# A ring of four slots instead of five for streamed weights

## The chip, the cores and the metric

The kernel runs on one core of one Trainium2 chip. The metric is the device time of one execution in microseconds (us). The kernel before was run three times: 1899.77, 1908.93 and 1909.86 us, median 1908.93.

## The reference

The layer mixes two branches, token by token: `out = g*a + (1-g)*b` with `g = sigmoid(sum(x * gate_w))`. Branch b is a feed-forward net with a gated GELU (2048 tokens of width 640, inner width 1536). Branch a is a recurrence over 64 segments of 32 tokens, and it is where the time goes:

```python
for s in range(n_seg):                      # 64 segments
    xs = x[:, s * seg_len:(s + 1) * seg_len, :].copy()
    h = jnp.concatenate([mem, xs], axis=1)  # 8 memory rows + 32 tokens
    q = jnp.einsum('btd,dhe->bhte', h, Wq)  # 32 heads of 192
    k = jnp.einsum('btd,dhe->bhte', h, Wk)
    v = jnp.einsum('btd,dhe->bhte', h, Wv)
    ...                                     # masked softmax
    o = jnp.einsum('bhqk,bhke->bhqe', p, v)
    o = jnp.einsum('bhte,hed->btd', o, Wo)
    mem = o[:, :M, :].copy()                # feeds the next segment
```

The eight memory rows of a segment come out of the segment before it, so segments can't overlap, and each of them reads all of Wq, Wk, Wv and Wo.

## The kernel before

**Stages.** First the feed-forward branch runs in four blocks of 512 tokens and leaves its rows in DRAM. Then the "left" stage (line 852) computes Q and K for the last eight tokens of each segment, for all segments at once. Then the 64 segments run one after the other; this is the recurrent stage, from about 316 us on.

**A segment.** The heads are treated in four octets. The list `PROG` gives the order of a segment's steps: `q`, `k` (line 931) and `v` (line 951) project an octet, `sc`, `ex` and `pt` compute scores, softmax and transposed probabilities, `pv` (line 1071) applies them to V, and `wo` (line 1094) multiplies with the rows of Wo and sums into one PSUM bank. At the end of a segment line 1139 copies the sum out, line 1149 transposes the new memory rows, and line 1154 puts them where the next segment's projections read them. An instruction scheduler written in Python (`_Sched`) turns declared reads and writes of memory regions into semaphore waits; each engine gets its operations in program order.

**Weights as pieces.** The four matrices don't fit into SBUF together, so they are cut into 84 pieces: 20 each of Wq, Wk and Wv (one 128-row slab for one octet, 128 x 3072 bytes, 384 KB) and 24 of Wo (two rows of 128, 128 x 2560 bytes, 320 KB). Below, "Q 0,3" is the Wq piece of octet 0, slab 3. Two pieces are held elsewhere (in PSUM, copied back on ACT at lines 610 and 623). The others are *resident* (loaded once, at line 647) or *streamed* (loaded again in each segment).

**Who is streamed.** A planner decides it when the kernel is built. It walks through `PROG` with a cost for each step (`COST`, in us) and so gives each piece a time of use. It then raises the number of streamed pieces, `nstream`, until the rest fits into `res_cap`, the bytes left after the work buffers and the ring. For each `nstream` it spreads target times evenly over a segment and takes for each target the allowed piece whose use lies nearest. One byte of the ring is one byte fewer for resident pieces:

```python
ring_bytes = B_RING * GQ                    # GQ = 3072 bytes a partition
res_cap = total - wsA_total - wsB_total - ring_bytes
```

**The ring.** Streamed pieces go through `B_RING` slots in turn. `issue_ring` (line 567) declares a DMA on the SP queue that writes slot `n % B_RING`. It has to wait until TensorE has finished with the piece that was in the slot before, and TensorE's matmuls wait for its landing. The SP queue is in order, and in the recurrent stage it carries nothing else but, in the first segment, late loads of resident pieces. The left stage passes ten pieces through the same slots (line 635). Other transfers, the rows of x, the left Q and K, b and the output, are issued by ACT (line 678 and 907).

In the kernel before, a segment streams 20 pieces through five slots: 4 of Wq, 5 of Wk, 3 of Wv and 8 of Wo.

Of the kernel before, what the change touches and what calls it, by code (L numbers as in the profile page):

```python
# [221 lines left out]
def _build(nc, A_x, A_mem0, A_Wq, A_Wk, A_Wv, A_Wo, seg_len, w_gate, w_up, w_down,  # L222
           gate_w, out, opts=None):
    opts = dict(opts or {})
# [81 lines left out]
    ffn_sz["brow"] = al(NBR * Dm * 2)  # L306
    ffn_total = sum(ffn_sz.values())

    B_RING = int(opts.get("ring", 5))
    ring_bytes = B_RING * GQ  # L310
    res_cap = total - wsA_total - wsB_total - ring_bytes
    assert total - wsA_total - ffn_total >= ring_bytes
# [7 lines left out]
    assert ffn_base >= ring_bytes  # L320
    ring_off = [j * GQ for j in range(B_RING)]
    o = wsA_base - wsB_total
# [137 lines left out]
    def piece_src(key):  # L460
        if key[0] == 3:
            r0, r1 = wo_row(2 * key[1]), wo_row(2 * key[1] + 1)
            return bass.AP(Wo2.tensor, Wo2.offset + r0 * Dm, [[3 * Dm, 128], [(r1 - r0) * Dm, 2], [1, Dm]])
        m, o_, k = key
        return (Wq2, Wk2, Wv2)[m][:, k, OW * o_:OW * (o_ + 1)]
# [4 lines left out]
    def piece_view(key, o):  # L470
        if key[0] == 3:
            return bview(o, GO).rearrange("p (c n) -> p c n", n=Dm)
        return bview(o, GQ)
# [55 lines left out]
    stream_list = [i for i in range(npieces) if i in streamed]  # L529
    assert nstream >= B_RING  # L530
    res_off = {}
# [30 lines left out]
    def issue_ring(seg, upto):  # L562
        done = issued.get(seg, 0)
        while done <= upto:
            key = order[stream_list[done]]
            slot = stream_counter[0] % B_RING
            S_.add("sp", lambda e, slot=slot, key=key: e.dma_start(piece_view(key, ring_off[slot]), piece_src(key)),
# [63 lines left out]
    def issue_left(upto):  # L631
        while len(left_slot) <= upto:
            key = left_stream[len(left_slot)]
            slot = stream_counter[0] % B_RING
            S_.add("sp", lambda e, slot=slot, key=key: e.dma_start(piece_view(key, ring_off[slot]), piece_src(key)),
                   writes=[r_ring[slot]], dma_sem="ring%d" % slot, name="ring left")
            stream_counter[0] += 1
            left_slot[key] = slot
# [11 lines left out]
    def load_residents(cls):  # L650
        for key in order:
            if key in res_off and slot_class[key] == cls:
                load_resident(key)
# [89 lines left out]
    def ffn_transposes(blk):  # L743
        s = blk % 2
        fns = []
        for a in range(FA):
            for k in range(KT):
                bank = k // 2
                col = (k % 2) * FB + a * 128
                fns.append(lambda e, a=a, k=k, bank=bank, col=col:  # L750
                           e.transpose(psb(bank)[:, col:col + 128], xr_sb[s][:, a, k * 128:(k + 1) * 128], ident))
        nb = (KT + 1) // 2
        S_.add("pe", fns, reads=[r_xr[s], r_ident], writes=[r_ps[b] for b in range(nb)], name="ffn xT %d" % blk)
        for bank in range(nb):
            k0 = 2 * bank
            nk = min(2, KT - k0)
            eng = "dve" if bank % 2 == 0 else "act"
            src = psb(bank)[:, 0:nk * FB].rearrange("p (k s t) -> p k s t", k=nk, t=L)
            dst = xT_sb[:, k0:k0 + nk]
            rk = [sreg(ffn_off["xT"] + 2 * k * L, 2) for k in range(k0, k0 + nk)]  # L760
            if eng == "dve":
                S_.add("dve", lambda e, src=src, dst=dst: e.tensor_copy(out=dst, in_=src),
                       reads=[r_ps[bank]], writes=rk)
            else:
                S_.add("act", lambda e, src=src, dst=dst: e.activation(out=dst, in_=src, func=ACTF.Copy),
                       reads=[r_ps[bank]], writes=rk)
        ns = FB // L
        aux_dma(xts[blk * ns:(blk + 1) * ns].rearrange("s p c -> p s c"),
                xT_flat.rearrange("p (s c) -> p s c", c=KT * L), r_xT, [Rg("xt", blk * ns, (blk + 1) * ns)], "xts")
# [50 lines left out]
    ffn_transposes(0)  # L820
    issue_left(min(B_RING, len(left_stream)) - 1)
    load_residents(0)
# [353 lines left out]
    for s in range(NSEG):  # L1176
# [5 lines left out]
                ring=B_RING, arena_bytes=arena_bytes,  # L1182
# [25 lines left out]
def bass_gated_mix__memory_aug_recurrent_mem_tr__glu_gated_geglu__prompt_kernel(  # L1208
    nc,
    A_x,  # L1210
    A_mem0,
    A_Wq,
    A_Wk,
    A_Wv,
    A_Wo,
    A_seg_len,
    B_x,
    B_w_gate,
    B_w_up,
    B_w_down,  # L1220
    gate_w,
    out,
):
    _build(nc, A_x, A_mem0, A_Wq, A_Wk, A_Wv, A_Wo, A_seg_len, B_w_gate, B_w_up, B_w_down, gate_w, out)
# [33 lines left out]
```

## Time and profile before

| what | value |
|---|---|
| profiled execution | 1908.93 us |
| its span, first to last instruction | 1907.2 us |
| mean granted TensorE clock | 0.983 |
| matmuls busy (PE) | 1762.1 us, 92% |
| weight loads busy (PEld) | 1126.8 us, 59% |
| VectorE, ScalarE busy | 929.6 us, 874.6 us |
| packets of the SP queue | 506.45 MB, 77.6% of 16 engines' span |
| packets of the ACT queue | 39.48 MB, 7.6% |

How to read it: the profile is one execution taken by the hardware profiler. PE and PEld are the matmuls and the weight loads of TensorE; both are fed by one sequencer. Matmuls are pipelined and their ends are modelled, so that PE counts as busy for longer than its array works. "Idle before" or "waited for" is an engine's idle time, put down to what ended it. In the chain of waits the program's last instruction is followed back, at each step to what released it. A DMA's landing is the moment when its last share has raised the semaphore. The time from issue to landing holds everything between, also the wait behind other transfers.

The transfers by origin in the page: Wo 528 issues of 320 KB, median 4.5 us to landing; Wk 340, Wq 277 and Wv 209 of 384 KB, 5.1, 4.9 and 5.1 us.

### The profile page before, as it was taken

What the parts mean: (1) busy time and instruction counts of PE and PEld (TensorE: products, weight loads), DVE (VectorE), ACT (ScalarE), POOL (GpSimd) and SP (SyncE); (2) the same over time, 40 slices, a digit from 0 to 9 for tenths busy, and PEclk for the clock granted to TensorE, in tenths of its full rate; (3) what the DMA queues carried; (4) which work ended last, traced back from release to release, by engine and by line L of the source; (5) the groups of instructions that cost most, each with busy time, mean ns of one, the idle gap of its engine ahead of it and who ended that gap; (6) DMA issues with size and microseconds to landing.
All of it is one profiled execution on the core that took longest, in us unless ns stands there. A gap on an engine that the chain in (4) does not pass through costs nothing.

```text
span 1907.2 us, 78849 instructions
## 1 busy us (share of the span) xinstructions
PE 1762.1 (92%) x34421; PEld 1126.8 (59%) x34429; DVE 929.6 (49%) x2890; ACT 874.6 (46%) x2045; POOL 145.1 (8%) x547
## 2 busy tenths in 40 slices
PE   7999995899999999999999999999999999999998
PEld 3454443566666666666666666666666566666665
DVE  3222332455555555555555555555555455545555
ACT  2222332444555454545454545455545444445554
POOL 1000000000000000000000000000000000000000
PEclk9999997999999999999999999999999999999999
DMA  9511567999999998999999999999999999999998
GB/s 373 196 35 41 153 162 247 329 310 314 304 304 326 304 325 301 322 311 331 312 317 308 308 309 331 311 327 313 321 307 324 301 315 310 308 308 316 325 319 276
DMA packets 280422, 550.98 MB, mean 289 GB/s; under 512 B 82434, under 2 KB 106506, under 8 KB 280074
## 3 DMA queue, kind: packets, MB, share of 16 engines
q1 hardware_dynamic: 201386, 506.45, 77.6%
q10 hardware_dynamic: 78688, 39.48, 7.6%
q8 instruction: 269, 4.41, 0.9%
q14 instruction: 79, 0.65, 0.1%
HBM read 524.69 MB, written 21.10 MB: 286 GB/s over the span
## 4 chain that ended last, share of the span: by engine, by line
PE 66%; DMA 24%; DVE 4%; ACTq 3%; issue 1%; ACT 1%; SPq 0%; DVEq 0%
PE ps L931 19%; DMA arena<-in_A_Wo_dram 13%; PE ps L1094 11%; PE ps L951 11%; DMA arena<-in_A_Wv_dram 5%; PE ps L852 4%; PE ps L1071 4%; DMA arena<-in_A_Wq_dram 4%; PE ps L993 3%; PE ps L785 3%; PE ps L782 3%; ACTq L867 2%; DMA arena<-in_A_Wk_dram 2%; PE ps L800 2%; PE ps L985 2%; PE ps L975 1%
## 5 line engine op out<-in xcount | busy, mean ns | idle before, releaser
L931 PE MATMUL ps<-arena 128*32 128x384 bf16 x10240 | 516.5, 334 | 29.2 <-DVE arena L1154 16.3
L1094 PE MATMUL ps<-arena 128*40 128x320 bf16 x6144 | 479.8, 300 | 30.6 <-DMA arena<-in_A_Wo_dram 26.3
L1094 PEld LDWEIGHTS ps<-arena 128*40 128x40 bf16 x6144 | 308.1, 100 | 135.8 <-DMA arena<-in_A_Wo_dram 65.7
L935 ACT ACTIVATE arena<-ps 128x384 bf16<-128x384 f32 x512 | 311.6, 609 | 148.6 <-PE ps L931 130.4
L931 PEld LDWEIGHTS ps<-arena 128*32 128x32 bf16 x10240 | 254.7, 98 | 173.1 <-DVE arena L1154 20.8
L951 PE MATMUL ps<-arena 128*32 128x384 bf16 x5800 | 294.6, 332 | 4.0 <-DMA arena<-in_A_Wv_dram 3.0
L941 DVE STREAM_TRANSPOSE arena<-arena 128x192 f32<-128x192 f32 x512 | 190.1, 371 | 120.8 <-ACT arena L935 120.2
L610 ACT ACTIVATE arena<-ps 128x576 bf16<-128x576 bf16 (+1 forms) x192 | 113.4, 590 | 234.7 <-PE ps L1094 231.7
L951 PEld LDWEIGHTS ps<-arena 128*32 128x32 bf16 x5800 | 147.6, 98 | 93.5 <-DMA arena<-in_A_Wv_dram 9.1
L962 ACT ACTIVATE arena<-ps 128x384 bf16<-128x384 f32 x256 | 125.6, 491 | 161.6 <-PE ps L951 79.5
L911 POOL COPY arena<-arena 128x96 bf16<-128x96 bf16 x256 | 68.4, 267 | 1555.6 <-PE ps L993 825.4
L1048 DVE TENSOR_TENSOR arena<-ps,arena 128x320 bf16<-128x320 bf16 x256 | 125.6, 491 | 114.7 <-PE ps L1045 112.8
L1020 ACT ACTIVATE ps<-ps 104x160 f32<-104x160 f32 x256 | 72.9, 285 | 176.8 <-DVE ps L1010 176.2
L1071 PEld LDWEIGHTS ps<-arena 128*64 128x64 bf16 x3072 | 113.0, 125 | 59.3 <-DVE ps L1010 25.8
L1075 ACT ACTIVATE arena<-ps 128x320 bf16<-128x320 f32 x256 | 111.7, 436 | 73.3 <-PE ps L1071 72.0
L1071 PE MATMUL ps<-arena 128*64 128x160 bf16 (+1 forms) x3072 | 136.4, 222 | 7.7 <-ACT arena L623 3.5
L1139 DVE CAST arena<-ps 104x320 bf16<-104x320 f32 x63 | 31.0, 492 | 228.5 <-PE ps L1094 228.5
L993 PE MATMUL ps<-arena 64*40 64x40 bf16 (+1 forms) x4096 | 120.6, 181 | 1.9 <-issue 1.7
L1008 DVE TENSOR_REDUCE arena<-ps 104x4 f32<-104x160 f32 x256 | 81.2, 317 | 72.2 <-PE ps L993 72.1
L852 PE MATMUL ps<-arena 128*128 128x512 bf16 x480 | 104.3, 380 | 4.2 <-ACT arena L859 4.2
L993 PEld LDWEIGHTS ps<-arena 64*40 64x40 bf16 (+1 forms) x4096 | 100.2, 97 | 11.5 <-issue 2.6
L1022 DVE TENSOR_REDUCE arena<-ps 104x4 f32<-104x160 f32 x256 | 82.3, 322 | 46.7 <-ACT ps L1020 27.7
(73 smaller groups left out, 1494.8 us busy)
## 6 DMA issues: line engine op xcount, KB each, us to landing
arena<-in_A_Wo_dram SPq DMA_DIRECT2D x528, 320.0 KB, 4.5
arena<-in_A_Wk_dram SPq DMA_DIRECT2D x340, 384.0 KB, 5.1
arena<-in_A_Wq_dram SPq DMA_DIRECT2D x277, 384.0 KB, 4.9
arena<-in_A_Wv_dram SPq DMA_DIRECT2D x209, 384.0 KB, 5.1
left_qk_scratch<-arena ACTq DMA_DIRECT2D x16, 768.0 KB, 8.1
arena<-left_qk_scratch ACTq DMA_DIRECT2D x64, 192.0 KB, 4.9
arena<-in_A_x_dram SPq DMA_DIRECT2D x4, 640.0 KB, 15.1
xt_scratch<-arena ACTq DMA_DIRECT2D x4, 640.0 KB, 9.1
```

Of the source, the lines that this page charges most:

```text
L610: S_.add("act", lambda e: e.activation(out=bview(o_held2, GQ)[:, c0:c1], in_=psb(b)[:, p0:p0 + c1 - c0], func=ACTF.Copy), reads=[r_ps[b]], ...
L852: S_.add("pe", [lambda e, k=k, g_=gs[k][0], i=i, bk=bk: e.matmul(ps[:, bk, 0:NL].rearrange("p (g t) -> p g t", t=L), g_[:, i * 128:(i + 1) ...
L931: S_.add("pe", [lambda e, j=j, k=k, gv=gv: e.matmul(ps[32 * j:32 * j + 32, bank, 0:384].rearrange("p (c i) -> p c i", i=32), Hb[hb][:, k, ...
L935: S_.add("act", lambda e: e.activation(out=rows_sb[m].rearrange("p (b i h) -> p b h i", b=6, h=2), in_=ps[:, bank, 0:384].rearrange("p (b ...
L941: S_.add("dve", lambda e: e.transpose(out=dst[:, :, 0:L], in_=rows_sb[m].bitcast(F32).rearrange("p (c r) -> p c r", r=L)), reads=[r_rows[m ...
L951: return [lambda e, j=j: e.matmul(ps[32 * j:32 * j + 32, bk, 0:384], lhs, g_[:, 384 * j:384 * (j + 1)], start=(k == 0), stop=(k == KT - 1) ...
L962: S_.add("act", lambda e: e.activation(out=v_sb[o % NVB], in_=ps[:, bank, 0:384], func=ACTF.Copy), reads=[r_ps[bank]], writes=[r_v[o % NVB ...
L993: fns.append(lambda e, gp=gp, lo=lo, hi=hi, b=(3 * tl + c) // 2, h=(3 * tl + c) % 2, tl=tl, last=(c != 1): e.matmul(ps[gp:gp + R, bank, tl ...
L1048: S_.add("dve", lambda e: e.tensor_tensor(out=PTm, in0=apx(pv[:, 0:104], [[64, 2], [0, 4], [1, R]]), in1=apx(mbd, [[0, 2], [1, 4], [0, R]] ...
L1071: fns.append(lambda e, lhs=lhs, left=left, h=h, dst=dst, rhs=rhs: e.matmul(dst, lhs, rhs, start=not left, stop=left, tile_position=(0, 64 ...
L1075: S_.add("act", lambda e: e.activation(out=apx(u[:, 0, 0, :], [[R, 2], [3 * R, 4], [1, R]]), in_=ps[:, A, 0:2 * W].rearrange("p (c t r) -> ...
L1094: fns.append(lambda e, g_=g_, i=i, c=c, h=h, tl=tl, cc=cc, u=u: e.matmul(ps[64 * h:64 * h + R, OB, 0:HD], u[:, tl, cc, :], g_[:, i, HD * h ...
```

## The change

The default number of ring slots goes from five to four. Nothing else in the text of the kernel changes; the planner, which computes with `ring_bytes`, then chooses another set of resident and streamed pieces, and slots follow in turns of four.

```diff
-    B_RING = int(opts.get("ring", 5))
+    B_RING = int(opts.get("ring", 4))
     ring_bytes = B_RING * GQ
     res_cap = total - wsA_total - wsB_total - ring_bytes
     assert total - wsA_total - ffn_total >= ring_bytes
```

The loop that the number feeds, unchanged:

```python
nstream = 0
while True:
    streamed = set()
    for k in range(nstream):
        target = (k + 0.5) * tseg / nstream
        best = min((i for i in range(npieces) if i not in streamed and i not in held_i and may_stream(order[i])), key=lambda i: abs(tcons[i] - target))
        streamed.add(best)
    if tot_bytes - GO - GQ - sum(piece_size(order[i]) for i in streamed) <= res_cap:
        break
    nstream += 1
```

The streamed pieces of a segment, in order of use:

| slots | pieces |
|---|---|
| five (20) | Q 0,3; K 0,4; Q 1,1; K 1,0; K 1,4; Q 2,3; K 2,1; V 2,0; Q 3,1; K 3,0; V 3,0; V 3,4; Wo 2, 5, 8, 11, 15, 18, 21, 23 |
| four (19) | Q 0,4; K 0,4; Q 1,2; K 1,1; Q 2,0; Q 2,4; K 2,3; V 2,2; Q 3,4; K 3,3; V 3,2; Wo 0, 5, 6, 11, 14, 18, 21, 23 |

## The prediction

> **What bounds the kernel now.** I read the page first: its span, engine shares and chain of waits.
>
> ```profile
> span 1907.2 us, 78849 instructions
> PE 1762.1 (92%) x34421; PEld 1126.8 (59%) x34429; DVE 929.6 (49%) x2890; ACT 874.6 (46%) x2045; POOL 145.1 (8%) x547
> ...
> PE 66%; DMA 24%; DVE 4%; ACTq 3%; issue 1%; ACT 1%; SPq 0%; DVEq 0%
> ```
>
> TensorE (PE) is nearly always busy, yet 24% of the chain is the flight of weight transfers. So weights arrive just in time. The busy time by stretches says whether bandwidth is short (columns end with granted clock, DMA share, GB/s):
>
> ```profile
> 0.00:50.00 50.00, 39.25 (x278) 19.27 (x280) 14.91 (x27) 12.81 (x19) 5.28 (x25) 1.00 0.99 374
> ...
> 345.00:1900.00 1555.00, 1457.19 (x32121) 974.57 (x32118) 832.66 (x2714) 780.06 (x1897) 134.71 (x504) 0.99 0.93 314
> ```
>
> The recurrent stage, 345 to 1900 us, is four fifths of the run. There the DMA engines look 0.93 occupied but move 314 GB/s; with a deep queue (first 50 us) they moved 374. So the stage uses 84% of a rate that this run shows. Next, the line that issues ring transfers: who waits for it, and issue to landing.
>
> ```profile
>   PEld ps L1094: 65.7, 124
>   PE ps L1094: 26.3, 42
>   PEld ps L931: 24.1, 40
>   PE ps L931: 10.9, 14
>   PEld ps L951: 9.1, 19
>   PEld ps L1071: 4.1, 6
>   PE ps L1071: 3.2, 5
>   PE ps L951: 3.0, 7
> ...
> DMA to landing us min/median/max: 3.1/4.8/10.6
> ```
>
> Matmuls idle 43.4 us for ring transfers, weight loads 103.0 us (partly covered by matmuls still running). The SP queue's own waits, and one piece of the chain, say why landings are late:
>
> ```profile
> SPq L567 <- PE ps L931: 299.4, 224, 17.0
> ...
> SPq L567 <- PE ps L1094: 178.8, 200, 1.8
> ```
>
> ```profile
> 1077.88 0.48 PE ps L931 x9
> 1078.36 6.04 DMA arena<-in_A_Wv_dram
> 1084.40 0.04 issue
> 1084.45 0.35 PE ps L951 x4
> ```
>
> SP waits for a matmul to finish with a slot, issues at once, and 6.04 us later TensorE goes on at the landing. The loop "slot freed, issue, landing, use" is what is tight. Last, the segment's length, from one instruction per segment:
>
> ```profile
> L1139 DVE CAST arena<-ps x63: 490/492/493, 352.2 to 1879.3; 104x320 bf16<-104x320 f32 x63
> ```
>
> (1879.3 - 352.2) / 62 = 24.63 us.
>
> **The change part by part.** By the planner's arithmetic (the issue counts of the page, 528 + 340 + 277 + 209 = 1354 = 64 x 20 + 10 + 62 + 2, confirm it for five slots) the 3072 bytes of the fifth slot make one more piece resident: 19 streamed instead of 20, 63 resident instead of 62. The streamed set is spread anew: 5 Wq, 4 Wk, 2 Wv, 8 Wo (was 4, 5, 3, 8).
>
> *Removed:* 64 SP issues of 0.33 us and 64 x 384 KB. SP spends its time waiting, so the issues are worth nothing. The bytes are hidden unless bandwidth is the bound (rival below). *Added:* one resident load, 384 KB at 374 GB/s = 1.1 us, issued while the FFN runs and the DMA share falls to 0.24 (50 to 180 us): nothing. If that cover were gone it would cost its 1.1 us. *Left stage:* ten left-row pieces pass the smaller ring, each needed two or more groups of about 13 us after its slot is free; landings there take 3.1 to 4.1 us: nothing.
>
> *Queues:* every ring issue now waits for the matmul four pieces back instead of five. Behind it on SP stand only further ring issues (and, in segment 0, late resident loads), so what is late is the landing, and TensorE waits for that. ACT's DMA queue and POOL are not passed.
>
> *The ring itself.* Average first. A slot's turn took 5/20 x 24.63 = 6.16 us; landing 4.8, reading 0.34 (Q, K, V) to 0.45 (Wo) and 0.09 for issue and semaphore make some 5.3, so 0.9 us was spare. With four slots a turn is 4/19 x 24.63 = 5.19 us: nothing is spare at the old landing time.
>
> Now piece by piece. From the instruction records I took, over segments 4 to 63, the median time from each piece's first matmul to the next one's where that one had landed 0.15 us early or more: a segment without ring stalls, 23.1 us. From it follows each streamed piece's window, from the last read of the piece before it in its slot to its own use. Windows with four slots, by turns of the ring (us):
>
> - Q, K, Q, K: 4.71, 4.44, 4.92, 5.59
> - Q, Q, K, V: 4.48, 4.32, 4.36, 4.42
> - Q, K, V, Wo: 4.22, 4.90, 4.87, 4.85
> - Wo x4: 4.95, 4.27, 4.44, 4.19
> - Wo x3: 3.92, 4.08, 3.18
>
> With five slots the shortest of the four turns were 5.26, 5.13, 5.43 and 3.99 (the last Wo piece).
>
> A landing plus 0.09 must fit the window; the largest excess in a turn is its stall (a stall early in a turn lengthens the later windows of the same turn, so they aren't added). Landings now average 4.95 (Q, K, V) and 4.52 (Wo): only 4.61 - 3.99 = 0.62 us per segment is overdue on average; the other 0.1 to 1.0 of the 0.7 to 1.6 measured (43.4 and 103.0 over 64) is scatter (standard deviation of a landing 0.63). I leave that scatter as it is.
>
> What will a landing take? Sorted by how many ring transfers were in flight at issue: four, 5.10 (Q, K, V) and 4.72 (Wo); three, 4.88 and 4.43; two, 4.13 and 4.31. With four slots a transfer meets three at most.
>
> - Slow end: the mean over three and fewer, 4.76 and 4.41. Stalls 0.41 + 0.53 + 0.63 + 0.31 + 1.32 = 3.20, or 2.58 more than 0.62; over 63 segments +163 us.
> - Fast end: the rows of two, 4.13 and 4.31. Stalls 0 + 0 + 0 + 0.21 + 1.22 = 1.43; +51 us.
> - Taken: 4.45, the middle, for Q, K, V, because "three in flight" in a ring of five often means that a fourth has just gone through the same engines; for Wo 4.27, a little under its row of two, because the Q, K, V transfers ahead of it thin out too. Stalls 0.10 + 0.22 + 0.32 + 0.17 + 1.18 = 1.99, so 1.37 more, x 63 = +86 us.
>
> The profiled execution took 1908.93 us (span 1907.2 and 1.7 around it), which is also the median of the three runs: 1908.9 + 86 = 1995 us.
>
> The Trainium skill ("Perfetto Trace Analysis", Identifying the Most-Contended Engine) judges a DMA by its HBM utilization and calls occupancy misleading. Read by occupancy, 0.93, the saved bytes would be worth the 69 us of the first rival; read by rate, 314 of 374 GB/s, they are worth nothing. The same skill ("DMA: Bandwidth & Descriptors", Anatomy of one DMA) gives 2.0 us plus bytes at 436 GB/s for a transfer issued from GpSimd; by that, an estimate, 384 KB land in 2.9 us, every window holds, and the sum would be -0.62 x 63 = -39 us. This trace's 4.8 us median speaks against it, its 3.1 us minimum for it.
>
> **The rivals.**
>
> *DMA bandwidth is the bound (faster).* For: share 0.93. Against: 314 against 374 GB/s, and SP waiting for TensorE before every issue. If so, the segment shortens by the removed transfer's engine time. A 3072-byte packet took 141 ns on average and each of 16 engines carries eight: 1.1 us, x 63 = -69, 1840 us. It decides where landings fall to 3.56 us: then the last window, 3.18, leaves 0.47 us of stall instead of 0.62, which is 9.5 us over 63 segments; for the full price they must come down to the 3.1 of a lone transfer.
>
> *Relief pays for the slot (same).* Landings of about 3.9 leave stalls of 0 + 0 + 0 + 0 + 0.81, near the 0.62 of now: +12 us, 1921; at 3.7, 1908. For: isolated transfers land in 3.1 to 3.3 us. Against: even with two in flight, 4.1 to 4.3.
>
> *No relief (slower still).* Landings stay 4.95 and 4.52: stalls 0.60 + 0.72 + 0.82 + 0.42 + 1.43 = 3.99, +3.37 x 63 = +212, 2121 us. For: the Wo row hardly moves with transfers in flight. Against: 5.4% fewer bytes over longer segments.
>
> *The planner doesn't drop a piece.* With 20 pieces in four slots a turn would be 4.93 us and the loss larger than forecast; the byte count excludes it.
>
> **How the numbers follow.** Ring starved as forecast: 0.82, between +51 and +163 us (1960 to 2072). No relief: 0.07. Relief pays: 0.06. Bandwidth: 0.05. The range 1945 to 2070 leaves out some 0.18 and a little of the forecast's slow end. About 0.5% (9.5 us) is what a measurement of this kernel can tell from no change: slower by more 0.91, within it 0.04, faster 0.05.
>
> **What would show it.** 1216 issues of the ring line; landing median 4.3 to 4.5 us; the segment from 24.63 to about 26.0 us; DMA rate falling to some 280 GB/s (7.73 MB a segment less 0.39, over 26.0); the waits of PE and its weight loads for weights about doubled, with more of them on Q and K pieces (line 931) and the longest on the last Wo pieces. Wrong: a landing median of 3.9 or less, a segment under 24.7 us, or a landing that stays at 4.8.

## The result and the profile after

The changed kernel is slower: 1972.11 us (median; 1965.88 to 1981.09) against 1904.35 us for the kernel before. The ratio is 1.0359, 95% interval 1.0303 to 1.0415. The forecast was 1995 us, 86 us more; measured are 68 us more. The profiled execution of the changed kernel took 1965.88 us, the shortest of its four, so its trace shows 57 us of them (span 1964.2 against 1907.2).

The page of the changed kernel, its span, engine shares and chain of waits:

```profile
span 1964.2 us, 78722 instructions
PE 1780.0 (91%) x34421; PEld 1114.1 (57%) x34429; DVE 928.9 (47%) x2890; ACT 878.2 (45%) x2045; POOL 145.1 (7%) x547
...
PE 55%; DMA 37%; DVE 4%; ACTq 2%; issue 1%; ACT 1%; SPq 0%; DVEq 0%
```

TensorE does the same work (34421 matmuls), and weight loads are even a little less busy. What has grown is the share of the chain that is a transfer in flight: 37% instead of 24%. That work hasn't moved to another engine; DVE, ACT and POOL are as they were.

Who waits for the ring's transfers, and the time from issue to landing:

```profile
  PEld ps L1094: 92.8, 150
  PEld ps L931: 89.4, 122
  PE ps L1094: 45.1, 76
  PE ps L931: 43.7, 70
  PEld ps L951: 11.0, 19
  PE ps L951: 3.9, 9
...
DMA to landing us min/median/max: 2.9/4.2/11.2
```

Matmuls idle 92.9 us for weights (43.4 before), weight loads 193.9 (103.0). The additional waits are above all at line 931, the Q and K projections: 43.7 us instead of 10.9. The landings themselves are shorter, 4.2 us in the median instead of 4.8. So a transfer is faster, and still later.

The length of a segment, and the busy time of the recurrent stage (columns as before: PE, weight loads, DVE, ACT, POOL, clock, DMA share, GB/s):

```profile
L1139 DVE CAST arena<-ps x63: 490/492/493, 354.7 to 1935.2; 104x320 bf16<-104x320 f32 x63
```

```profile
345.00:1900.00 1555.00, 1421.21 (x31042) 928.85 (x31042) 802.66 (x2617) 754.73 (x1825) 130.07 (x487) 0.99 0.89 288
```

A segment takes (1935.2 - 354.7) / 62 = 25.49 us, 0.86 more than 24.63; 62 of them make 53 of the 57 us. The other 4 us lie before the first of these rows (354.7 instead of 352.2) and behind the last; one execution of each kernel doesn't tell whether that is more than chance. The DMA rate fell from 314 to 288 GB/s, at the same clock.

One place of the chain, with the loop of the forecast in it:

```profile
1076.10 0.53 PE ps L931 x13
1076.63 4.95 DMA arena<-in_A_Wk_dram
1081.58 0.04 issue
1081.63 0.51 PE ps L931 x8
```

Matmuls of line 931 free a slot at 1076.63, SP issues the next transfer into it, and 4.95 us later matmuls of the same line go on at its landing. Before, a fifth slot stood between the two.

### The profile page after: what moved, and what is told of

Read it like the earlier page. It is cut to its first block, busy times and chain, and to the rows that moved or that the text cites. A ratio compares the mean times of both kernels' runs of the same rounds, so it can differ in the third digit from the quotient of the medians.

```text
span 1964.2 us, 78722 instructions
## 1 busy us (share of the span) xinstructions
PE 1780.0 (91%) x34421; PEld 1114.1 (57%) x34429; DVE 928.9 (47%) x2890; ACT 878.2 (45%) x2045; POOL 145.1 (7%) x547
## 4 chain that ended last, share of the span: by engine, by line
PE 55%; DMA 37%; DVE 4%; ACTq 2%; issue 1%; ACT 1%; SPq 0%; DVEq 0%
DMA arena<-in_A_Wo_dram 17%; PE ps L931 16%; DMA arena<-in_A_Wq_dram 10%; PE ps L1094 9%; PE ps L951 9%; DMA arena<-in_A_Wk_dram 8%; PE ps L852 4%; PE ps L1071 3%; PE ps L785 3%; PE ps L782 3%; PE ps L993 2%; ACTq L867 2%; DMA arena<-in_A_Wv_dram 2%; PE ps L800 2%; PE ps L975 1%; PE ps L1149 1%
## 5 line engine op out<-in xcount | busy, mean ns | idle before, releaser
L931 PE MATMUL ps<-arena 128*32 128x384 bf16 x10240 | 525.2, 333 | 61.7 <-DMA arena<-in_A_Wq_dram 27.4
L1094 PE MATMUL ps<-arena 128*40 128x320 bf16 x6144 | 486.4, 301 | 49.7 <-DMA arena<-in_A_Wo_dram 45.1
L931 PEld LDWEIGHTS ps<-arena 128*32 128x32 bf16 x10240 | 249.6, 98 | 228.2 <-DMA arena<-in_A_Wq_dram 56.5
L951 PE MATMUL ps<-arena 128*32 128x384 bf16 x5800 | 296.1, 332 | 4.2 <-DMA arena<-in_A_Wv_dram 3.9
L951 PEld LDWEIGHTS ps<-arena 128*32 128x32 bf16 x5800 | 146.3, 98 | 95.1 <-DMA arena<-in_A_Wv_dram 11.0
L1071 PE MATMUL ps<-arena 128*64 128x64 bf16 (+1 forms) x3072 | 136.2, 223 | 3.7 <-ACT arena L623 2.7
```

What stands on the lines that cost most here:

```text
L931: S_.add("pe", [lambda e, j=j, k=k, gv=gv: e.matmul(ps[32 * j:32 * j + 32, bank, 0:384].rearrange("p (c i) -> p c i", i=32), Hb[hb][:, k, ...
L951: return [lambda e, j=j: e.matmul(ps[32 * j:32 * j + 32, bk, 0:384], lhs, g_[:, 384 * j:384 * (j + 1)], start=(k == 0), stop=(k == KT - 1) ...
L1071: fns.append(lambda e, lhs=lhs, left=left, h=h, dst=dst, rhs=rhs: e.matmul(dst, lhs, rhs, start=not left, stop=left, tile_position=(0, 64 ...
L1094: fns.append(lambda e, g_=g_, i=i, c=c, h=h, tl=tl, cc=cc, u=u: e.matmul(ps[64 * h:64 * h + R, OB, 0:HD], u[:, tl, cc, :], g_[:, i, HD * h ...
```

## The experiments

My theory: a transfer can leave only when its slot is free, and that moment, the window before its use and the landing time decide. The rivals: bandwidth is the bound; the other choice of pieces does it, not the ring; the saved transfer is worth nothing. All runs were compared with the kernel before on the same chip.

**The ring alone.** Four slots, but the pieces of the kernel before.

```diff
-    B_RING = int(opts.get("ring", 5))
+    B_RING = int(opts.get("ring", 4))
...
-    nstream = 0
+    nstream = 20
```

> Four slots, but the 20 streamed pieces of the kernel before (3072 bytes a partition stay unused): the ring alone, without the saved transfer. Theory (slots starve TensorE): a slot's turn shrinks from 6.16 to some 5.1 us; landings fall to about 4.5 (Q, K, V) and 4.2 us (Wo), as in the changed kernel; ring stalls per segment about 3.1 us instead of 1.5, so some 100 to 125 us more than before: 2005 to 2030 us, clearly slower than the changed kernel's 1972. Rival (bandwidth is the bound and slots matter little): the bytes are those of before, so is the time, within 1%. Rival (the new set of pieces causes the loss, not the ring): time of before.

Measured: 2038.0 us, ratio 1.0685 (1.0618 to 1.0753), 135 us more than the 1903.3 of the kernel before beside it. A little over the theory's range; both rivals fall. Its page and its ring line:

```profile
PE 47%; DMA 46%; DVE 3%; ACTq 2%; issue 1%; ACT 1%; SPq 0%; DVEq 0%
```

```profile
  PEld ps L1094: 127.4, 204
  PEld ps L931: 90.3, 123
  PE ps L1094: 63.7, 106
  PE ps L931: 51.1, 65
...
DMA to landing us min/median/max: 2.6/4.3/10.8
```

```profile
L1139 DVE CAST arena<-ps x63: 491/492/493, 357.6 to 2006.9; 104x320 bf16<-104x320 f32 x63
```

A segment takes (2006.9 - 357.6) / 62 = 26.60 us. The bytes of a segment are those of before, the landings those of the changed kernel: means of 4.44 us (Q, K, V) and 4.14 (Wo), in the changed kernel 4.42 and 4.14. With four slots, then, the shorter landing comes from the missing slot, not from the missing bytes.

**The saved transfer alone.** Five slots and 19 pieces; one resident piece isn't kept and another is read in its place.

```diff
+    ALIAS = {(1, 0, 1): (1, 0, 0)}
-    nstream = 0
+    nstream = 19
-        if tot_bytes - GO - GQ - sum(piece_size(order[i]) for i in streamed) <= res_cap:
+        if tot_bytes - GO - 2 * GQ - sum(piece_size(order[i]) for i in streamed) <= res_cap:
```

> Five slots and the changed kernel's 19 streamed pieces: the saved transfer alone. There is no room for both, so one resident piece isn't kept: the K projection of octet 0 uses slab 0 of Wk in place of slab 1, with the same instructions. Theory: a turn is 5/19 of a segment, 6.3 us, and every window but the last two holds; ring stalls fall from 1.5 to some 0.6 to 1.0 us a segment, 30 to 55 us less than before: 1850 to 1875 us. Rival (bandwidth): 69 us less, 1835. Rival (the saved transfer is hidden anyway): no change, 1904.

Measured: 1847.48 us, ratio 0.9681 (0.9631 to 0.9731), 56 us less than before. The theory's range missed it by 3 us, the bandwidth rival by 12; what tells them apart is in the profile:

```profile
  PEld ps L1099: 19.8, 43
  PEld ps L936: 11.9, 14
  PE ps L936: 6.8, 5
  PE ps L1099: 6.8, 14
...
DMA to landing us min/median/max: 3.1/4.5/10.6
```

```profile
345.00:1810.00 1465.00, 1401.58 (x31580) 968.94 (x31572) 818.20 (x2666) 762.08 (x1860) 132.55 (x496) 1.00 0.93 311
```

```profile
L1144 DVE CAST arena<-ps x63: 491/492/493, 352.8 to 1817.8; 104x320 bf16<-104x320 f32 x63
```

A segment takes (1817.8 - 352.8) / 62 = 23.63 us. Waits for the ring have nearly gone (matmuls 15 us instead of 43) at 311 GB/s, and other runs below move 318 to 342 GB/s, so the rate was not at its limit. The gain is above all a longer turn of the slots; landings also became shorter (means of 4.70 and 4.31 us instead of 4.94 and 4.53). The two halves of the change thus are: one slot less, +135 us; one transfer less, -56 us with five slots and 2038 - 1972 = -66 us with four. The slot is worth some two times the transfer that it was given for. (The choice of pieces changes with their number in these pairs; a run below shows 12 us from another choice alone.)

**The floor.** The ring is loaded in segment 0 alone.

```diff
-            S_.add("sp", lambda e, slot=slot, key=key: e.dma_start(piece_view(key, ring_off[slot]), piece_src(key)),
-                   writes=[r_ring[slot]], dma_sem="ring%d" % slot, name="ring s%d p%d" % (seg, done))
+            if seg == 0:
+                S_.add("sp", lambda e, slot=slot, key=key: e.dma_start(piece_view(key, ring_off[slot]), piece_src(key)),
+                       writes=[r_ring[slot]], dma_sem="ring%d" % slot, name="ring s%d p%d" % (seg, done))
```

> Five slots; the ring is loaded in segment 0 alone, and later segments read whatever lies in the slots (the weights of the streamed pieces are then wrong ones). This is the floor of the recurrent stage, without ring stalls. Theory: the segment falls from 24.63 to the 23.1 us summed from stall-free pieces, 93 us less: about 1812 us. Rival (DMA traffic also slows the matmuls or their clock): below 1790. Rival (less is lost to the ring than the records say, the waits being covered by other work): above 1850.

Measured: 1820.89 us, ratio 0.9539 (0.9468 to 0.9611).

```profile
L1140 DVE CAST arena<-ps x63: 491/492/493, 354.5 to 1794.0; 104x320 bf16<-104x320 f32 x63
```

A segment without ring transfers takes (1794.0 - 354.5) / 62 = 23.22 us. The 23.1 us that were summed from the records of before hold. The windows hold too: taken from this trace piece by piece (from the end of the last matmul of the piece before in the slot, means over segments 4 to 63), those of four slots differ from the forecast's list by 0.14 us at most. Ring stalls are thus 24.63 - 23.22 = 1.41 us a segment before and 2.27 after.

**How stalls add up.** Four slots, 19 pieces, with the Wo pieces at the end of a segment moved so that two summing rules differ.

```diff
-    B_RING = int(opts.get("ring", 5))
+    B_RING = int(opts.get("ring", 4))
...
+    FORCED = [(0, 0, 4), (1, 0, 4), (0, 1, 2), (1, 1, 1), (0, 2, 0), (0, 2, 4), (1, 2, 3), (2, 2, 2), (0, 3, 4), (1, 3, 3), (2, 3, 2), (3, 0), (3, 5), (3, 6), (3, 9), (3, 11), (3, 14), (3, 18), (3, 21)]
+    streamed = {order.index(key) for key in FORCED}
```

> Four slots and 19 pieces as in the changed kernel, but the streamed Wo pieces are 0 5 6 9 11 14 18 21 instead of 0 5 6 11 14 18 21 23. The last windows are then 4.95 4.27 3.90 3.05 2.83 3.27 3.14 us instead of 4.85 4.95 4.27 4.44 4.19 3.92 4.08 3.18 (with Wo 0 ahead of them in both). Theory A, as the prediction summed it (the largest excess of each turn, turns added): 1.40 for the last turn and 1.18 for the one before it instead of 1.05 and 0.04, 1.5 us a segment more than the changed kernel, +94 us: some 2065. Theory B (a stall lengthens all later windows that span it, also those of the next turn, so the delay of piece n is the larger of the delay of n-1 and that of n-4 plus landing minus window): 0.4 to 0.5 us a segment more, +23 to +34 us: 1995 to 2006.

Measured: 1994.82 us (1983.4 to 2008.4), ratio 1.0454 (1.0383 to 1.0524); a segment takes (1964.5 - 352.7) / 62 = 26.00 us.

```profile
L1144 DVE CAST arena<-ps x63: 491/492/493, 352.7 to 1964.5; 104x320 bf16<-104x320 f32 x63
```

That is 0.51 us more than in the changed kernel, where theory A expected 1.5 and theory B 0.4 to 0.5: B holds, and the rule of the prediction (A) is refuted. (Moving the last Wo piece forward also lengthens the windows of the next segment's first pieces; the sums of the next section contain that.)

**The other side: six slots.**

```diff
-    B_RING = int(opts.get("ring", 5))
+    B_RING = int(opts.get("ring", 6))
```

> Six slots; the planner then streams 22 pieces, 8.1 MB a segment instead of 7.3. The other side of the trade. Theory (latency with a bandwidth limit behind it): windows grow to 5.3 to 7.0 us but for the last two (4.7), landings grow with the queue to 5.3 to 6 us, DMA rate to some 335 GB/s; 0.3 to 0.7 us a segment more than before, +20 to +45 us: 1924 to 1948. Rival (slots alone count, the queue costs nothing): landings stay at 4.9 and 4.5, stalls nearly vanish, 1830 to 1860. Rival (bandwidth is a hard limit at the 374 GB/s of the first 50 us): 8.1 + 0.4 MB at 374 GB/s is 22.8 us a segment, so the time isn't limited by it.

Measured: 1919.41 us, ratio 1.0079 (1.0047 to 1.0111): slower, by less than expected. Landings rose to 5.48 us (Q, K, V) and 5.06 (Wo), the rate to 342 GB/s:

```profile
345.00:1810.00 1465.00, 1371.05 (x30190) 917.04 (x30184) 783.65 (x2547) 733.73 (x1779) 127.05 (x473) 0.99 0.97 342
```

```profile
L1139 DVE CAST arena<-ps x63: 490/492/493, 355.1 to 1888.2; 104x320 bf16<-104x320 f32 x63
```

A segment takes (1888.2 - 355.1) / 62 = 24.73 us. The rival with unchanged landings falls. A slot more is no longer worth the two transfers that its bytes cost. Five is the best of the three.

**A better spread.** Five slots, 20 pieces chosen so that fewer windows are short (the list of the expectation: 13 of Q, K, V and 7 of Wo).

> Five slots and 20 pieces (12 of Wq, Wk, Wv and 8 of Wo) as in the kernel before, but another choice, Q 0,0; Q 0,2; K 0,4; Q 1,3; K 1,4; Q 2,0; Q 2,3; K 2,3; V 2,2; Q 3,3; K 3,1; V 3,0; V 3,4; Wo 2 5 8 11 14 20 23, with Q, K, V 13 and Wo 7. It is chosen so that fewer windows are shorter than a landing (the three Wo pieces 15, 18, 21 of the tail become 14 and 20). Theory (only windows against landings count): ring stalls fall by some 0.3 to 0.45 us a segment, 19 to 28 us less than before: 1875 to 1885 us. Rival (the planner's even spread by its costs is as good, since the same number of slots turns): 1904 within 0.5%.

Measured: 1891.84 us, ratio 0.9929 (0.9902 to 0.9956): faster, by half of what was expected. The waits at Wo fell, those at Q and K rose:

```profile
  PEld ps L936: 67.3, 122
  PE ps L936: 27.1, 52
  PEld ps L956: 24.6, 40
  PEld ps L1099: 20.3, 34
```

```profile
L1144 DVE CAST arena<-ps x63: 490/492/493, 352.7 to 1874.7; 104x320 bf16<-104x320 f32 x63
```

A segment takes (1874.7 - 352.7) / 62 = 24.55 us here; but the profiled execution, 1902.68 us, was the slowest of seven. Landings had become longer too, 5.06 us for Q, K, V instead of 4.94. That a TensorE which stalls less asks faster, so that the queue gives part of the gain back, would fit; no run shows it apart from the other choice of pieces.

**A slot from bytes that are free for half a segment.** One streamed Wo piece is loaded into the row buffers and the staging of the left Q and K, which nobody uses late in a segment. It takes no turn of the ring.

```diff
+    OVL = (3, 15)
...
+        if key == OVL:
+            S_.add("sp", lambda e: e.dma_start(piece_view(key, o_ovl), piece_src(key)), writes=[r_ovl], dma_sem="ovl",
+                   name="ovl s%d" % seg)
+            return piece_view(key, o_ovl), r_ovl
...
-    o_held = wsB_off["rows"] + al(2 * 768) - GO
+    o_held = wsB_off["Q"]
+    o_ovl = o_held + GO
...
-        elif s + 1 < NSEG:
-            stg_load(s + 1)
...
                 wo_part(s, item)
+                if item == ("wo", 2) and s + 1 < NSEG:
+                    stg_load(s + 1)
```

> Five slots, 19 pieces through the ring and a twentieth, Wo 15, loaded in each segment into bytes that are free in the last half of it (the row buffers and the staged left Q and K, 2560 bytes, 128 of them new); the other held Wo piece moves down to the start of Q, and the next segment's left Q and K are loaded after Wo 15 is read instead of after the last scores. All weights are the right ones. The ring's windows are those of five slots with 19 pieces, the bytes those of 20. Theory: 0.55 to 0.85 us a segment less than before, 34 to 53 us: 1850 to 1870 us, between the changed number of pieces alone (1847) and the better spread alone. Rival (bytes were what the 19-piece run gained): 1904, or what the spread alone gives. Rival (the later load of left Q and K delays the first scores of a segment): above 1904.

Measured: 1873.08 us, ratio 0.9829 (0.98 to 0.9857), 31 us less than before and 3 us over the expected range. It changed two things, overlay and spread, so the overlay was run with the old spread too:

> The overlay of the run before (Wo 15 loaded into the free row buffers and staging, not through the ring), but with the other 19 streamed pieces as the kernel before has them, so that the spread is not changed with it. All weights are the right ones. Its windows are 6.51 6.67 5.58 5.99 6.08 5.13 5.33 5.41 5.36 6.03 5.95 5.60 5.81 5.43 5.43 4.86 6.26 5.55 5.32 us: the three short ones at the end of a segment (4.74 4.74 3.99) are gone. Theory: what counts is windows against landings (5.2 and 4.6 us as with the other overlay, plus 0.09); none is overdue on average but K 2,3's neighbour by 0.1 to 0.2; stalls of 0.7 to 0.9 us a segment from scatter, 0.5 to 0.7 less than before: 1860 to 1875 us, as good as the overlay with the new spread (1873). Rival (the new spread brought that run's gain): 1890 to 1904.

Measured: 1865.33 us (1862.27 to 1869.36), ratio 0.9786 (0.9759 to 0.9813), within the expected range: the best version, 2.1% faster than the kernel before with all of its weights. The overlay makes the gain, not the spread. Its segment and its waits:

```profile
L1151 DVE CAST arena<-ps x63: 491/492/492, 354.5 to 1837.9; 104x320 bf16<-104x320 f32 x63
```

```profile
  PEld ps L943: 22.4, 53
  PEld ps L1104: 18.5, 47
...
DMA to landing us min/median/max: 3.0/4.9/11.1
```

(1837.9 - 354.5) / 62 = 23.93 us, 0.71 over the floor, half of the stalls of before, though 20 transfers run and land as late as ever (4.9 us). Wo (line 1104 here) has lost most of its waits: 18.5 us of weight loads instead of 65.7.

## Why the prediction was right, and where it was off

- **What bounds.** Right. DMA bandwidth had room (six slots moved 342 GB/s), and the loop "slot freed, issue, landing, use" was the limit: the ring alone costs 135 us at unchanged bytes.
- **Landing time.** Taken were 4.45 us for Q, K, V and 4.27 for Wo, measured are 4.42 and 4.14. The numbers came close, the rule behind them less so. Of the Q, K, V transfers of the changed kernel (from 450 us on) 486 met three others at issue, 151 two and 12 one; with these shares the rows of before give 4.69 us. Taking the middle of two rows instead was a judgement, and partly luck. Three in flight now meant 4.46 us instead of 4.88. The reason that I gave beforehand, a fourth transfer just gone, doesn't explain this: in the trace of before, transfers with three in flight took 5.04 us where another had landed less than 0.3 us earlier (93 of them), and still 4.80 us otherwise (170). What tells the two kernels apart is the number in flight over a transfer's whole flight: with three at issue, a Q, K, V transfer had 3.04 others beside it on average with five slots and 2.39 with four. Where that average lay between 2.25 and 2.75, it took 4.52 us in both kernels.
- **The removed transfer.** "The issues are worth nothing" and "the bytes are hidden" hold for bandwidth; but the transfer was worth 56 to 66 us through the turn of the slots. The sum contained this, since its windows were those of 19 pieces; the text, which put the transfer at nothing, should have said so.
- **The step that failed: the sum of stalls.** It took the largest excess of each turn of the ring and added the turns: 1.99 us a segment, a growth of 1.37 over the 0.62 of before. But the windows of the first pieces of a turn span the last pieces of the turn before; a stall there lengthens them too. The delay of piece n is the larger of the delay of piece n-1 and of the delay of the piece before it in its slot plus landing plus 0.09 minus window. With the forecast's own landings this gives 1.66 instead of 1.99; with the measured ones 1.37. What comes on top, which the prediction took for scatter and left as it was, is 2.27 - 1.37 = 0.90 after and 1.41 - 0.63 = 0.78 before. So the forecast growth of 1.37, less 0.33 for double counting and 0.29 for shorter landings, plus some 0.1 of what comes on top, is 0.86 us: the measured growth of a segment. The mechanism was right and this term too large, by three fifths in the two profiled executions; by the medians of all executions, 86 us forecast and 68 measured, by a quarter.

Both rules, worked out with the mean landings of each run (from 450 us on), against the measured stall (segment less 23.22), in us per segment. Two columns go a step further. "Each segment's windows" takes the windows of every segment from the trace of the floor run, since every fourth segment has additional matmuls; "own landings" also takes each transfer's own landing from the run's trace instead of the mean (segments 8 to 63):

| run | landing Q,K,V / Wo | turns added | delays chained | chained, each segment's windows | and own landings | measured |
|---|---|---|---|---|---|---|
| before, 5 slots, 20 | 4.94 / 4.53 | 0.63 | 0.63 | 0.69 | 1.12 | 1.41 |
| changed, 4 slots, 19 | 4.42 / 4.14 | 1.65 | 1.37 | 1.61 | 2.07 | 2.27 |
| 4 slots, 20 | 4.44 / 4.14 | 2.50 | 2.25 | 2.60 | 3.11 | 3.38 |
| 5 slots, 19 | 4.70 / 4.31 | 0 | 0 | 0 | 0.33 | 0.41 |
| 4 slots, tail moved | 4.35 / 4.16 | 2.96 | 1.68 | 1.74 | 2.59 | 2.78 |
| 5 slots, new spread | 5.06 / 4.56 | 0.12 | 0.12 | 0.27 | 1.12 | 1.33 |
| 6 slots, 22 | 5.48 / 5.06 | 0.76 | 0.76 | 0.78 | 1.08 | 1.51 |

Chained delays lie 0.4 to 1.2 us under the measurement everywhere; added turns lie above it with the tail moved. Except with six slots, the largest part of that gap is the scatter of landings (standard deviation 0.57 to 0.74 us in these runs): with own landings the chain comes within 0.1 to 0.3 us, with six slots within 0.4. What this rest is stays open. The prediction carried the scatter over from before at an unchanged size and didn't work it out; that is the open part of the method.

- **Rivals.** Bandwidth (1840 us) and "no relief" (2121 us) fell with the landings, which came down by half a microsecond and not to 3.56, and with the time itself. The price of the bandwidth rival, 69 us, didn't fit the prediction's own sum: with 0.62 us of stall a segment, landings of 3.1 us could have given 38 us at most, because the sum left the scatter as it was. "Relief pays for the slot" needed landings of 3.9. The estimate from "DMA: Bandwidth & Descriptors" in the Trainium skill (Anatomy of one DMA), 2.9 us for 384 KB and so a gain, lies below every ring transfer of that size in the changed kernel (3.1 us at least). The rule of "Perfetto Trace Analysis" (Identifying the Most-Contended Engine) to go by rate and not by occupancy was borne out: at a share of 0.93 the DMA engines moved 314 GB/s, and with six slots 342.
- **Signs.** Issues fell from 1280 to 1216 as forecast; the segment, 25.49 against 26.0 us, and the rate, 288 against 280 GB/s, follow from the smaller stall. Waits of PE and its weight loads rose by factors of 2.1 and 1.9 ("about doubled"), most of it on Q and K. Two signs were missed in part: the median landing, 4.2 us, lies just under "4.3 to 4.5", and the longest waits were not all on the last Wo pieces. Over segments 4 to 63 the matmuls idled 15.6 us before Wo 23, the last, but 13.0 before Wo 14 and only 1.4 and 3.2 before Wo 18 and 21.

## What to carry to other kernels

For a ring of prefetch slots, write down each transfer's window, from the last read of the slot to the use, and compare it with the landing time under load; chain the delays instead of adding excesses, and allow for the scatter of landings, which in the kernel before cost 0.43 us a segment beside 0.69 for landings that are late in the mean. The average turn doesn't decide whether a slot can be given up: here it was 5.19 us or more, longer than a mean landing of 4.3 with reading and issue (some 4.8 together), and yet the slot cost 135 us and bought 66. Look first for memory that is idle where the windows are shortest: 2560 such bytes gained more than any of the three sizes of the ring.

## What was not expected of the hardware

- **Landing time followed the transfers in flight, and so the number of slots.** It was 4.4, 4.9 and 5.5 us for 384 KB with four, five and six slots, with 2.3, 3.1 and 3.9 other weight transfers beside it on average. The bytes of a segment counted less: with four slots it was the same at 20 pieces as at 19, with five 4.9 and 4.7. A transfer with nothing else in flight took 3.1 (issued at 252.2 us in the run of the floor).
- **Busy DMA engines say little.** From before to after the rate fell by 8% (314 to 288 GB/s) and the occupied share by 4% (0.93 to 0.89): the median 3072-byte packet stayed at 121 ns, but the mean rose from 141 to 149. Packets that start while few others run are recorded as longer: in the changed kernel 276 ns on average with fewer than eight others under way, 134 with sixteen or more. At a share of 0.93 there was room: six slots moved 342 GB/s at 0.97.
